# A one-tile expert slot turned and moved, and a port shared by two engines put into a planner's estimates

## The chip, the core and the metric

One core of a Trainium2 chip runs the whole program. Its engines are TensorE (PE, matmuls, with PEld for its weight loads), VectorE (DVE), ScalarE (ACT), GpSimd (POOL) and SyncE (SP, which issues most transfers). The metric is the device time of one execution in microseconds (us); the median of several runs is compared.

## The reference

Three stages, all in float32, each on the output of the one ahead of it:

```python
# 1. linear attention with decay, 4 x 8 heads, 768 steps, 48 wide
cur = einsum('bhd,bhe->bhde', u * kt, vt)
y[:, :, t] = einsum('bhd,bhde->bhe', rt, state + cur)
state = w * state + einsum('bhd,bhe->bhde', kt, vt)
# 2. a dense layer on the 3072 tokens of width 384
h = x @ w_in                      # 384 x 2048
x2 = (h * sigmoid(h)) @ w_out     # 2048 x 384
# 3. each token goes to one of 8 experts (the largest logit)
e_idx = argmax(x2 @ w_gate + modality_bias[modality_id], axis=1)
out[mask] = gate_w * (relu(x2[mask] @ w1[e]) @ w2[e])   # 384 x 1024, 1024 x 384
```

## The kernel before

Every product of stages 2 and 3 is made from three float32r matmuls: a value is split into a high part (h) and the rest (l), and hi*hi, hi*lo and lo*hi are added up. So each product needs ACT for the high part and DVE for the subtraction that gives the low one: xh and xl for inputs, Wh and Wl for weights, gh and gl for the hidden values.

The 3072 tokens are 24 tiles of 128. Attention works tile by tile: POOL makes zb (L448) and scales the keys by a table (L464), DVE scales the queries (L460), PE makes the sums c (L454) and the scores (L487), the output y (L503) and the state (L544). Three tiles make a block of 384 tokens for the dense layer. That has 16 chunks of the hidden width; for a chunk the **first product** is nine matmuls of 384 columns (L618), then ACT takes Silu twice (L622, L623), DVE makes gl (L625), and the **second product** is nine matmuls (L637) into three PSUM banks, one for each tile. While the first two blocks run, the dense weights are converted chunk by chunk on ACT and DVE (L587 to L596). A tile's logits are then computed, tokens are sorted into lists by expert, and rows go to DRAM.

Stage 3 works in nine static **slots**, each with one expert's weights: SP loads them, ACT and DVE split them (L925, L929), POOL gathers the tokens' rows (L915), PE transposes them (L933), and a slot makes 8 first products (L949) with Relu on ACT (L1034) and gl on DVE (L1036), and 8 second products (L957). At its end, outputs are scaled by the gate on DVE and ACT (L963, L961), and POOL writes each tile of 128 rows by an indirect transfer (L966). Eight slots hold 384 tokens; the last, ninth one holds 128 tokens (one tile) and makes its first products in two groups of 36 matmuls of 128 columns. A loop behind them takes what did not fit into the slots (L1079; it does not run here).

What sets the order: `Plan` (L57) collects all operations with an engine, an estimated duration, a priority and dependencies, and `order` (L75) plays them through as a list scheduler: whenever an engine is free in its estimate, the ready operation of least priority starts. The resulting order is written out as it is, and each engine takes its instructions in that order. PSUM banks and buffers are handed out in the same pass. Where the planner finds PE free in the first 150 us of its own estimate, it places a **filler**: four transposes of the identity matrix (L372), which compute nothing that is used. No estimate says that DVE and POOL can hinder each other.

Of the kernel before, what the change touches and what calls it, by code (L numbers as in the profile page):

```python
# [31 lines left out]
NA = 4  # L32
# [20 lines left out]
class Op:  # L53
    __slots__ = ("eng", "dur", "prio", "fn", "deps", "acq", "rel", "lat", "nbytes", "start", "n", "left", "after", "slots")


class Plan:  # L57
# [7 lines left out]
    def add(self, eng, dur, prio, fn, deps=(), acq=(), rel=(), lat=0.2, nbytes=0):  # L65
        o = Op()
        o.eng, o.dur, o.prio, o.fn, o.lat, o.nbytes = eng, dur, prio, fn, lat, nbytes
        o.deps = [d for d in deps if d is not None]
        o.acq, o.rel = list(acq), list(rel)
        o.n, o.after, o.left = len(self.ops), [], 0  # L70
        self.ops.append(o)
        return o

    def order(self):
# [5 lines left out]
        busy = dict.fromkeys(ENGINES, 0.0)  # L80
        events, dma, t, done = [], 0.0, 0.0, []
# [4 lines left out]
        while True:  # L86
            moved = True
            while moved:
                moved = False
                for e in ENGINES:  # L90
# [20 lines left out]
                    busy[e] = t + o.dur  # L111
                    end = t + o.dur + o.lat
                    if o.nbytes:
                        dma = max(dma, t + o.dur) + o.nbytes / 260e3
                        end = dma + 3.8 + o.lat
# [24 lines left out]
def moe_rwkv_kernel(tc, ins, out):  # L140
# [267 lines left out]
    def attention(n):  # L408
# [25 lines left out]
        if n >= NZ:  # L434
            o_pr = add("POOL", 1.2, z - 3.3, lambda: gp.tensor_tensor(nat(0), nat(0), nat(1), op=ALU.mult), [oB])
            o_pu = add("POOL", 1.2, z - 3.0, lambda: gp.tensor_tensor(nat(0), nat(0), UW, op=ALU.mult), [o_pr, o_ul])
# [5 lines left out]
        else:  # L442
# [6 lines left out]
            o_z = add("POOL", 1.4, z - 4, f_z, [oA], acq=[("zb", kz)])  # L449
# [10 lines left out]
        o_r = add("DVE", 0.62, z - 3.0, lambda: vv.tensor_tensor(*scale(0), op=ALU.mult), zd)  # L460
        if n < 3:
            o_k = add("DVE", 0.62, z - 3.0, lambda: vv.tensor_tensor(*scale(1), op=ALU.mult), zd)
        else:
            o_k = add("POOL", 1.4, z - 3.2, lambda: gp.tensor_tensor(*scale(1), op=ALU.mult), zd)  # L464
# [14 lines left out]
        if not last:  # L479
            o_kk = add("POOL", 1.2, z - 2.0, lambda: gp.tensor_tensor(nat(1), nat(1), PKt, op=ALU.mult), [o_pr or oB, o_pk])  # L480
# [65 lines left out]
        if c > 0:  # L546
            st = Sst[b].rearrange("p q a d -> p q (a d)")
            o_sw = add("POOL", 0.95, z - 0.5, lambda: gp.tensor_tensor(st, st, wc.unsqueeze(2).to_broadcast([128, 4, 2 * D]),
                                                                      op=ALU.mult), [sdone[n - B], o_y])
# [21 lines left out]
    def convert(fc):  # L571
# [12 lines left out]
        def cx():  # L584
# [6 lines left out]
                 [o1])  # L591
        o4 = add("DVE", 0.95, z + 0.3, lambda: vv.scalar_tensor_tensor(cx(), cx(), 0x80000000, st_(1),
                                                                      op0=ALU.bitwise_and, op1=ALU.bitwise_or), [o3])
# [578 lines left out]
```

## Time and profile before

| | us |
|---|---|
| median of 3 runs | 781.47 (779.93 to 781.54) |
| the profiled execution | 780.16 |
| its span, from the first to the last instruction | 778.4 |
| PE busy | 763.3 (98%) |
| DVE busy | 400.1 (51%) |
| ACT busy | 341.8 (44%) |
| POOL busy | 214.1 (28%) |

The span starts with the first instruction and ends with the last, and 1.8 us of the execution lie around it. Times in the rows are us from the start of the span. A busy share near 100% says that PE has hardly a gap, and not that what it does is needed: the fillers count as busy. The mean granted clock of TensorE is 0.994 of full speed, so there is a short stretch in which it was lower.

### The profile page before, as it was taken

Reading aid. Unit: us, or ns where it says so; the run is one execution under the profiler, and the core shown is the slowest. Engines: PE = TensorE matmul, PEld = TensorE weight load, DVE = VectorE, ACT = ScalarE, POOL = GpSimd, SP = SyncE. Lnnn points to the kernel's source line nnn. Section 1 sums busy time; section 2 is a strip of 40 time slices with the busy share of each in tenths; the row PEclk is TensorE's granted clock in tenths of the full one; section 3 lists DMA queues with packets and bytes.
Section 4 is the critical chain, followed back from the end, with each engine's and each line's share of the span. In section 5 each row is a group of like instructions: output and inputs, shape, how many; then the busy total and the mean of one; then the engine's idle time right before and its main releaser. Section 6 shows DMA issues by size and latency. Waiting matters only on the chain. (4 is left out here: it accounts for less than half of the span.)

```text
span 778.4 us, 15275 instructions
## 1 busy us (share of the span) xinstructions
PE 763.3 (98%) x6104; PEld 733.9 (94%) x6104; DVE 400.1 (51%) x793; ACT 341.8 (44%) x742; POOL 214.1 (28%) x276
## 2 busy tenths in 40 slices
PE   8989999999999999999999999999999999999996
PEld 7988999999999999999999999999999999999995
DVE  7978985545434433433533442245685455455521
ACT  4756775444434334333433432335643354334410
POOL 4324300343512522342141120321241322222102
PEclk9989999999999999999999999999999999999999
DMA  7625441244311311311022040915265653350000
GB/s 248 217 98 186 167 153 34 89 77 78 92 61 62 93 62 61 93 61 62 24 90 82 22 32 1 377 39 193 82 184 184 223 182 133 133 203 27 11 21 36
DMA packets 23918, 83.24 MB, mean 107 GB/s; under 512 B 7659, under 2 KB 12152, under 8 KB 21538
## 3 DMA queue, kind: packets, MB, share of 16 engines
q1 hardware_dynamic: 19730, 72.55, 28.9%
q0 software_dynamic: 3968, 9.66, 3.7%
q8 instruction: 49, 0.80, 0.5%
q14 instruction: 27, 0.22, 0.2%
q10 hardware_dynamic: 144, 0.00, 0.0%
HBM read 78.92 MB, written 9.77 MB: 114 GB/s over the span
## 5 line engine op out<-in xcount | busy, mean ns | idle before, releaser
L625 DVE TENSOR_TENSOR gl<-sg,gh 128x384 fp32r<-128x384 f32 x128 | 81.0, 633 | 154.5 <-ACT gh L623 146.6
L622 ACT ACTIVATE sg<-ph 128x384 f32<-128x384 f32 x128 | 62.9, 491 | 205.5 <-PE ph L618 187.8
L637 PE MATMUL pa<-Wh,gh 128*128 128x384 f32 x384 | 133.1, 347 | 0.0
L637 PE MATMUL pa<-Wh,gl 128*128 128x384 f32 x384 | 130.0, 338 | 1.2 <-DVE gl L625 1.2
L637 PE MATMUL pa<-Wl,gh 128*128 128x384 f32 x384 | 129.3, 337 | 0.0
L618 PE MATMUL ph<-xh,Wh 128*128 128x384 f32 x384 | 92.9, 350 | 0.0
L618 PE MATMUL ph<-xh,Wl 128*128 128x384 f32 x384 | 88.8, 339 | 0.0
L618 PE MATMUL ph<-xl,Wh 128*128 128x384 f32 x384 | 88.5, 338 | 0.0
L1034 ACT ACTIVATE gh<-ph 128x384 fp32r<-128x384 f32 (+1 forms) x66 | 32.6, 494 | 113.5 <-PE ph L949 107.2
L1036 DVE SCALAR_TENSOR_TENSOR gl<-ph,gh 128x384 fp32r<-128x384 f32 (+1 forms) x66 | 36.8, 558 | 81.2 <-ACT gh L1034 80.4
L637 PEld LDWEIGHTS pa<-Wh,gh 128*128 128x128 f32 x384 | 72.5, 189 | 3.6 <-issue 2.2
L637 PEld LDWEIGHTS pa<-Wh,gl 128*128 128x128 f32 x384 | 72.6, 189 | 1.5 <-DVE gl L625 1.5
L637 PEld LDWEIGHTS pa<-Wl,gh 128*128 128x128 f32 x384 | 72.6, 189 | 0.0
L618 PEld LDWEIGHTS ph<-xh,Wh 128*128 128x128 f32 x384 | 66.2, 189 | 4.4 <-issue 3.0
L475 ACT ACTIVATE atall<-ident,cs 128x128 f32<-128x128 f32 x192 | 62.0, 397 | 18.9 <-DVE cs L457 10.5
L618 PEld LDWEIGHTS ph<-xl,Wh 128*128 128x128 f32 x384 | 69.5, 189 | 0.0
L618 PEld LDWEIGHTS ph<-xh,Wl 128*128 128x128 f32 x384 | 69.5, 188 | 0.0
L929 DVE TENSOR_TENSOR Wl<-raw,Wh 128x1024 fp32r<-128x1024 f32 (+2 forms) x54 | 64.0, 1219 | 9.9 <-ACT Wh L925 9.9
L966 POOL DMA_INDIRECT out_dram<-x2all,it x25 | 33.8, 1354 | 126.6 <-DVE x2all L963 114.7
L957 PE MATMUL pa<-Wh,gh 128*128 128x384 f32 x200 | 67.5, 337 | 1.0 <-DVE x2all L963 0.8
L957 PE MATMUL pa<-Wh,gl 128*128 128x384 f32 x200 | 67.4, 337 | 0.0
L957 PE MATMUL pa<-Wl,gh 128*128 128x384 f32 x200 | 67.0, 335 | 0.0
(225 smaller groups left out, 1285.9 us busy)
## 6 DMA issues: line engine op xcount, KB each, us to landing
raw<-in_we_dram SPq DMA_DIRECT2D x18, 1536.0 KB
AB<-in_av_dram SPq DMA_DIRECT2D x18, 768.0 KB
stall<-in_wio_dram SPq DMA_DIRECT2D x16, 768.0 KB
x_rows<-x2all SPq DMA_DIRECT2D x24, 192.5 KB
AB<-y_slow SPq DMA_DIRECT2D x16, 256.0 KB
stall<-in_av_dram SPq DMA_DIRECT2D x5, 768.0 KB
AB<-in_rk_dram SPq DMA_DIRECT2D x10, 384.0 KB
stall<-in_rk_dram SPq DMA_DIRECT2D x5, 384.0 KB
```

The lines of the kernel that those rows point to most:

```text
L475: act.activation(atb[sl_(kT)][h % 2][:, h // 2, :], ident, AF.Copy, scale=cs[:, h:h + 1])
L618: pe.matmul(p, win(a, fc, kt), (xh, xl)[b_][j % 2][:, kt, :], start=i == 0, stop=i == len(ops) - 1)
L622: o_s = add("ACT", 0.5, s - 4, lambda: act.activation(sgb[sl_(kS)], hps[sl_(kH)][:, 0:n], AF.Silu), [o_g1], acq=[("sg", kS)])
L625: o_l = add("DVE", 0.55, s - 4, lambda: vv.tensor_tensor(glb[sl_(kG)][:, 0:n], sgb[sl_(kS)], ghb[sl_(kG)][:, 0:n].bitcast(F32), op=ALU.sub ...
L637: pe.matmul(a, g[:, ts], wout(wp_, fc), start=begin and i == 0, stop=end and i == 2)
L929: eng.tensor_tensor(e_view(buf, 1)[wi][sl], m2[s]["raw", wi][sl], e_view(buf, 0)[wi][sl].bitcast(F32), op=ALU.subtract)
L957: pe.matmul(a[:, 0:DM], g[:, sl], wt_[:, fc, :], start=fc == 0 and m == 0, stop=fc == NFE - 1 and m == 2)
L966: i = gp.indirect_dma_start(out=out, out_offset=bass.IndirectOffsetOnAxis(ap=m2[s]["it"][:, t:t + 1], axis=0), in_=o, in_offset=None, boun ...
L1034: o2 = add("ACT", 0.62 if small else 0.5, z + k - 6, lambda kH=kH, kG=kG, m=m: act.activation(ghb[sl_(kG)][:, 0:m], hps[sl_(kH)][:, 0:m], ...
L1036: o3 = add("DVE", 0.7 if small else 0.57, z + k - 6, lambda kH=kH, kG=kG, m=m: vv.scalar_tensor_tensor(glb[sl_(kG)][:, 0:m], hps[sl_(kH)][ ...
```

## The change

Three things are done. In `Plan`, an operation can be marked `shared`; when it starts while a marked operation of the other of the two engines DVE and POOL is running in the estimate, its duration there grows by half of the overlap. Marked are the elementwise operations on DVE and POOL of attention, of the weight conversions and of the gl subtraction in the dense layer, and the weight splits of the experts.

The one-tile slot moves from the last place to the one ahead of it (`small` is slot 7 in place of 8), and takes its list entry with it. Its first product is turned: the tokens are the stationary operand and 512 columns of the weights stream past, nine matmuls for half of the hidden width. The result has tokens on partitions, so Relu goes to a tile `hn` in SBUF, PE transposes it in four parts, ACT copies the high part and DVE makes gl.

In the slot that is now the last, the second products of the last two chunks wait for both and are added tile by tile, so that a tile's output need not wait for the other two. The marks alone (`shared=True` at 14 places) are shown at one place:

```diff
@@ order
+        run = dict.fromkeys(ENGINES, 0.0)
...
-                    busy[e] = t + o.dur
-                    end = t + o.dur + o.lat
+                    dur = o.dur
+                    if o.shared:
+                        other = run["POOL" if e == "DVE" else "DVE"]
+                        if other > t:
+                            dur += 0.5 * min(dur if e == "POOL" else 2 * dur, other - t)
+                        run[e] = t + dur
+                    busy[e] = t + dur
+                    end = t + dur + o.lat
@@ attention
-            o_z = add("POOL", 1.4, z - 4, f_z, [oA], acq=[("zb", kz)])
+            o_z = add("POOL", 1.4, z - 4, f_z, [oA], acq=[("zb", kz)], shared=True)
@@ new helpers
+    def e_g1n(buf, xb, k, p):
+        w1h, w1l = e_view(buf, 0)[0], e_view(buf, 1)[0]
+        ops = [(kt, a, b_) for b_, a in ((xh, w1h), (xh, w1l), (xl, w1h)) for kt in range(KT)]
+        for m, (kt, a, b_) in enumerate(ops):
+            pe.matmul(p, b_[xb][:, kt, 0:128], a[:, kt, k * 512:(k + 1) * 512], start=m == 0, stop=m == len(ops) - 1)
+
+    def e_tn(g, p):
+        for i in range(4):
+            pe.transpose(p[:, i * 128:(i + 1) * 128], g[:, i * 128:(i + 1) * 128], ident)
@@ swap
+        pools["hn"] = [ew.tile([128, 512], F32, name=f"hn{i}") for i in range(1)]
@@ expert
-        z = E0 + EU * s
+        z = E0 + EU * s if s < NSTAT - 1 else E0 + EU * (s - 1) + 2.0
-        small = s == NSTAT - 1
+        small = s == NSTAT - 2
+        final = s == NSTAT - 1
+        at_ = NSTAT - 1 if small else NSTAT - 2 if final else s
...
+            if small:
+                kN = ("en", s, k)
+                o1 = add("PE", 2.1, z + k, lambda k=k, kH=kH: e_g1n(buf, xb, k, hps[sl_(kH)]), [o_sp[0, p_] for p_ in range(3)] + o_x,
+                         acq=[("h", kH)])
+                o2 = add("ACT", 0.62, z + k - 6, lambda kH=kH: act.activation(
+                    pools["hn"][0], hps[sl_(kH)], AF.Relu), [o1], rel=[kH])
+                o2 = add("PE", 0.45, z + k - 6, lambda kN=kN: e_tn(pools["hn"][0], tps[sl_(kN)]), [o2], acq=[("t", kN)])
+                o2 = add("ACT", 0.62, z + k - 6, lambda kG=kG, kN=kN: act.activation(ghb[sl_(kG)], tps[sl_(kN)], AF.Copy), [o2],
+                         acq=[("g", kG)])
+                o3 = add("DVE", 0.7, z + k - 6, lambda kG=kG, kN=kN: vv.tensor_tensor(
+                    glb[sl_(kG)], tps[sl_(kN)], ghb[sl_(kG)].bitcast(F32), op=ALU.subtract), [o2], rel=[kN])
...
+            if final and fcs[0] >= NFE - 2:
+                held = [] if fcs[0] == NFE - 2 else held
+                held.append((kG, need))
+                if fcs[0] == NFE - 1:
+                    both = [d for _, ds in held for d in ds]
+                    for t in range(nt_):
+                        def f_g2(t=t):
+                            for i, (kq, _) in enumerate(held):
+                                e_g2(buf, [NFE - 2 + i], t, n, ghb[sl_(kq)], glb[sl_(kq)], aps[sl_(ka[t])])
+                        lastg = last_t[t] = add("PE", 1.05, z + k + 2.3 + 0.1 * t, f_g2, both + [lastg], rel=[kq for kq, _ in held] if t == nt_ - 1 else [])
+                continue
```

What this does to the order is seen at three places. Names in the rows are the program's: pt, ph and pa are PSUM banks, AB_132 the inputs of attention tile 3 and AB_133 those of tile 4, gh_121 and gh_122 the hidden values of chunks 0 and 1. Behind the change, line numbers up to the expert's helpers are 8 higher.

PE, where the second product of chunk 0 ends and attention tile 3 begins (L454 makes c, L487 the scores, L618 is the first product of chunk 3, L637 the second product of chunk 1), before:

```order
L637 MATMUL pa_80<-Wh_73,gl_124 128x384
L454 MATMUL pt_83<-ub,zb_134 128x2 x4
L487 MATMUL pt_82<-AB_132 128x128
L487 MATMUL pt_84<-AB_132 128x128
...
L454 MATMUL pt_83<-ub,zb_135 128x2 x4
L618 MATMUL ph_78<-xh_115,Wh_73 128x384 x3
...
L637 MATMUL pa_81<-Wh_73,gh_122 128x384
```

And with the change (L380 are the fillers, L645 the second product, L462 makes c, L495 the scores, L626 is the first product of chunk 2):

```order
L645 MATMUL pa_80<-Wh_73,gl_124 128x384
L380 MATMUL ph_78<-ident 128x128 x4
L380 MATMUL ph_77<-ident 128x128 x4
...
L645 MATMUL pa_79<-Wh_73,gh_122 128x384
...
L462 MATMUL pt_83<-ub,zb_134 128x2 x4
L495 MATMUL pt_84<-AB_132 128x128
...
L626 MATMUL ph_77<-xh_115,Wh_73 128x384 x3
...
L380 MATMUL ph_78<-ident 128x128 x12
L462 MATMUL pt_83<-ub,zb_135 128x2 x4
```

Five fillers and the second product of chunk 1 now stand ahead of tile 3, and three more fillers between the tiles 3 and 4. In all, 49 fillers are written out in place of 39.

DVE at the same place, from the conversion of chunk 3 (L590, L592, L594, L596 on cx_148) to the scaling of tile 3's queries (L460), before:

```order
L590 TENSOR_SCALAR stall<-cx_148 128x768
L592 SCALAR_TENSOR_TENSOR cx_148<-cx_148,stall 128x768
L625 TENSOR_TENSOR gl_124<-sg_119,gh_121 128x384
L594 ISA cx_148<-stall,cx_148 128x1536
L625 TENSOR_TENSOR gl_125<-sg_120,gh_122 128x384
L460 TENSOR_TENSOR AB_132<-AB_132,Pt 128x512
```

And with the change (all line numbers 8 higher):

```order
L633 TENSOR_TENSOR gl_124<-sg_119,gh_121 128x384
...
L633 TENSOR_TENSOR gl_125<-sg_120,gh_122 128x384
L604 TENSOR_TENSOR Wl_75<-cx_147,Wh_73 128x768
L468 TENSOR_TENSOR AB_132<-AB_132,Pt 128x512
L465 TENSOR_SCALAR cs_480<-pt_83,flag 128x8
L598 TENSOR_SCALAR stall<-cx_148 128x768
L600 SCALAR_TENSOR_TENSOR cx_148<-cx_148,stall 128x768
L602 ISA cx_148<-stall,cx_148 128x1536
```

The gl of chunks 0 and 1 and the queries of tile 3 have come ahead of the conversion of chunk 3.

PE in the one-tile slot, with the change (L964 is its first product, L968 the transposes, L957 the first product of the last slot, L975 second products, the last row here the slot's own):

```order
L964 MATMUL ph_77<-Wh_74,xh_116 128x512 x3
...
L975 MATMUL pa_81<-Wh_73,gh_123 128x384
...
L964 MATMUL ph_78<-Wh_74,xh_116 128x512 x3
...
L968 MATMUL pt_82<-ident,hn_5340 128x128 x4
L975 MATMUL pa_81<-Wh_73,gh_121 128x384
...
L968 MATMUL pt_83<-ident,hn_5340 128x128 x4
L957 MATMUL ph_77<-xh_115,Wh_73 128x384 x3
...
L975 MATMUL pa_80<-Wh_74,gh_122 128x384
```

Before, this slot's 72 narrow matmuls stood at the end of the program, with the second products of the full slot before it between and behind them; now its pieces stand between the products of the full slots on either side.

## Rows read from the trace of the kernel before

**Rows 1.** Stretches: us, busy us (count) of PE, PEld, DVE, ACT, POOL; granted clock; DMA.

```profile
44.00:50.00 6.00, 5.58 (x34) 5.42 (x32) 4.63 (x9) 3.25 (x9) 1.00 (x1) 0.63 0.29 109
76.00:80.00 4.00, 2.85 (x17) 2.64 (x16) 3.96 (x6) 3.70 (x8) 0.88 (x1) 1.00 0.65 240
150.00:552.00 402.00, 401.62 (x3486) 381.09 (x3487) 163.86 (x397) 158.96 (x405) 113.62 (x147) 1.00 0.27 81
```

**Rows 2.** Waits of PE, whole span: us in total, times, longest.

```profile
PE pt L487 <- issue: 1.6, 1, 1.6
PE pa L637 <- DVE gl L625: 1.2, 1, 1.2
```

**Rows 3.** Timeline of PE around 45 us: start, duration, instruction, idle before it.

```profile
41.22 0.95 PE L454 MATMUL pt<-ub,zb 128*128 128x2 f32 x8
...
45.31 1.59 PE L454 MATMUL pt<-ub,zb 128*128 128x2 f32 x8 [0.42 <-DVE cs L457]
46.77 1.31 PE L618 MATMUL ph<-xh,Wh 128*128 128x384 f32 x3
...
49.79 0.52 PE L637 MATMUL pa<-Wh,gh 128*128 128x384 f32 x1
...
52.65 1.08 PE L503 MATMUL pt<-atall,AB 128*32 128x128 f32 x32
```

**Rows 4.** Timeline of PE at a run of four fillers.

```profile
73.82 2.03 PE L372 MATMUL ph<-ident 128*128 128x128 f32 x16
75.61 0.42 PE L637 MATMUL pa<-Wh,gh 128*128 128x384 f32 x1
```

**Rows 5.** Timelines of POOL and DVE, one overlapping pair.

```profile
35.92 1.48 POOL L464 TENSOR_TENSOR AB<-AB,Qt 128x512 f32<-128x512 f32 x1
...
36.30 1.92 DVE L592 SCALAR_TENSOR_TENSOR cx<-cx,stall 128x768 uint32<-128x768 uint32 x1
```

**Rows 6.** DVE by form, 0 to 90 us (busy, mean ns), and two alone.

```profile
L625 DVE TENSOR_TENSOR gl<-sg,gh 128x384 fp32r<-128x384 f32 x9 | 9.2, 1024 | 1.6 <-ACT gh L623 1.6
L590 DVE TENSOR_SCALAR stall<-cx 128x768 uint32<-128x768 uint32 x10 | 8.5, 855 | 0.6 <-ACT cx L587 0.6
...
22.48 0.58 DVE L590 TENSOR_SCALAR stall<-cx 128x768 uint32<-128x768 uint32 x1
...
44.42 0.55 DVE L625 TENSOR_TENSOR gl<-sg,gh 128x384 fp32r<-128x384 f32 x1
```

**Rows 7.** Timeline of PE at the end, the one-tile slot among it.

```profile
752.02 0.69 PE L949 MATMUL ph<-xh,Wh 128*128 128x384 f32 x3
...
753.61 0.33 PE L957 MATMUL pa<-Wh,gh 128*128 128x384 f32 x1
...
755.16 0.44 PE L949 MATMUL ph<-xh,Wh 128*128 128x128 f32 x3
...
759.13 0.39 PE L957 MATMUL pa<-Wh,gh 128*128 128x384 f32 x1
...
766.15 0.34 PE L957 MATMUL pa<-Wh,gl 128*128 128x384 f32 x1
766.63 0.45 PE L957 MATMUL pa<-Wh,gh 128*128 128x384 f32 x1
...
770.73 0.34 PE L957 MATMUL pa<-Wh,gl 128*128 128x384 f32 x1
```

**Rows 8.** Timeline of DVE: the splits for the last slot, and a gl of it.

```profile
729.83 3.50 DVE L929 TENSOR_TENSOR Wl<-raw,Wh 128x1024 fp32r<-128x1024 f32 x3 [0.39 <-ACT Wh L925]
...
759.96 0.69 DVE L1036 SCALAR_TENSOR_TENSOR gl<-ph,gh 128x512 fp32r<-128x512 f32 x1 [5.08 <-ACT gh L1034]
```

**Rows 9.** Timeline of POOL: the last output transfers.

```profile
768.32 0.99 POOL L966 DMA_INDIRECT out_dram<-x2all,it  x1 [0.24 <-issue]
...
769.62 0.99 POOL L966 DMA_INDIRECT out_dram<-x2all,it  x1 [0.24 <-issue]
...
772.01 0.98 POOL L966 DMA_INDIRECT out_dram<-x2all,it  x1 [1.34 <-DVEq L1079]
```

More of the change, by code (lines that the diff above doesn't have):

```diff
@@ L53 @@
 class Op:
-    __slots__ = ("eng", "dur", "prio", "fn", "deps", "acq", "rel", "lat", "nbytes", "start", "n", "left", "after", "slots")
+    __slots__ = ("eng", "dur", "prio", "fn", "deps", "acq", "rel", "lat", "nbytes", "start", "n", "left", "after", "shared")
 class Plan:
@@ L1030, in expert @@
             m = n * step
-            o1 = add("PE", 2.7 if small else 1.57, z + k * (1.0 if small else 1.0), lambda fcs=fcs, kH=kH: e_g1(buf, xb, fcs, n, hps[sl_(kH)]),
-                     [o_sp[0, p_] for p_ in range(3)] + o_x, acq=[("h", kH)])
-            em["g1", s] = em["g1", s] + [o1]
-            o2 = add("ACT", 0.62 if small else 0.5, z + k - 6, lambda kH=kH, kG=kG, m=m: act.activation(
-                ghb[sl_(kG)][:, 0:m], hps[sl_(kH)][:, 0:m], AF.Relu), [o1], acq=[("g", kG)])
-            o3 = add("DVE", 0.7 if small else 0.57, z + k - 6, lambda kH=kH, kG=kG, m=m: vv.scalar_tensor_tensor(
-                glb[sl_(kG)][:, 0:m], hps[sl_(kH)][:, 0:m], 0.0, ghb[sl_(kG)][:, 0:m].bitcast(F32), op0=ALU.max, op1=ALU.subtract),
-                [o2], rel=[kH])
@@ L1039, in expert @@
-            need = [o_sp[1, p_] for p_ in range(((0, 0, 0, 1, 1, 1, 2, 2)[fcs[-1]]) + 1)] + [o3, lastg]
+            if small:
[9 more added lines that the diff above has]
+                    glb[sl_(kG)], tps[sl_(kN)], ghb[sl_(kG)].bitcast(F32), op=ALU.subtract), [o2], rel=[kN])
+            else:
+                o1 = add("PE", 1.57, z + k * 1.0, lambda fcs=fcs, kH=kH: e_g1(buf, xb, fcs, n, hps[sl_(kH)]),
+                         [o_sp[0, p_] for p_ in range(3)] + o_x, acq=[("h", kH)])
+                em["g1", s] = em["g1", s] + [o1]
+                o2 = add("ACT", 0.5, z + k - 6, lambda kH=kH, kG=kG, m=m: act.activation(
+                    ghb[sl_(kG)][:, 0:m], hps[sl_(kH)][:, 0:m], AF.Relu), [o1], acq=[("g", kG)])
+                o3 = add("DVE", 0.57, z + k - 6, lambda kH=kH, kG=kG, m=m: vv.scalar_tensor_tensor(
+                    glb[sl_(kG)][:, 0:m], hps[sl_(kH)][:, 0:m], 0.0, ghb[sl_(kG)][:, 0:m].bitcast(F32), op0=ALU.max, op1=ALU.subtract),
+                    [o2], rel=[kH])
@@ L1049, in expert @@
             o5 = add("ACT" if t == 1 else "DVE", 0.55, z + 1 + 0.1 * t, f_o,
[L1050 removed]
+                     [last_t.get(t, lastg), em.get(("out", s - 2))] + ([routed["sx", NB - 1]] if s < 2 else []), rel=[ka[t]])
             em["out", s] = add("POOL", 1.0, z + 7 + 0.1 * t, lambda t=t: e_out(s, t, x2b[s % 2][:, t, 0:DM]), [o5], lat=5.0)
```

36 lines of the change are left out of this document (18 added, 18 removed).

## The prediction

> **What bounds the kernel now.** I read the windows first: they say where TensorE (PE) is the bound. From 150 to 552 us PE is busy 401.62 of 402 us at full clock [rows 1], so there nothing that ACT, DVE or POOL do shows in the time, and whatever is won or lost on PE before 150 us or behind 700 us is carried to the end one to one. Next the waits of PE. Apart from short ones far behind, where the change leaves the order as it is, PE waits in three places, all before 90 us: 1.6 us ahead of the score matmuls of attention tile 3, 0.42 us ahead of the small matmuls of tile 4, and 1.2 us for a gl [rows 2, 3]. That sum is 3.2 us. Then the timeline of PE around the first two: behind them it runs slowly. [...] Waits and slow clock together cost **6.45 us** in the first 90 us. Everything else there is PE work, and a part of that work is padding: fillers of four transposes each that the planner puts where it believes PE would idle.
>
> Why PE waits at 43 us is seen on DVE and POOL. A POOL multiply runs from 35.92 to 37.40; the DVE operation that begins inside it, at 36.30, takes 1.92 us [rows 5], about 0.97 more than the 0.95 that the plan writes for it. The plan of before knows nothing of this. Over the first 90 us the two forms that lose most are the gl subtraction (9 of them, mean 1024 ns against 0.55 us alone) and the shift of the weight conversion (10, mean 855 ns against 0.58 us) [rows 6]: 9 x 0.47 + 10 x 0.275 = 7.0 us of DVE time that no estimate held.
>
> **The change, part by part.** (1) The estimates. An operation marked as sharing is charged half of its overlap with the other engine's running one. For the pair above the overlap is 1.10 us, so the table now charges 0.55 of the 0.97 that the row shows: 57%. The order that comes out has the same operations, with the second product of chunk 1 moved ahead of tile 3's attention matmuls (they open with c and the scores), and with 49 fillers in place of 39. A group of 16 filler matmuls goes from 73.82 to 75.61 us [rows 4], 0.112 us each; 10 fillers are 40 of them, **4.47 us** more PE work, all before 150 us and so all on the path. From there to the last expert slots the order of PE is the same row by row.
>
> What it can give back is the 6.45 us. Fillers keep PE busy where it now waits, and they let tile 3 come later against its producers. What of it stays is the one unknown; I call it x, the PE waits and slow-clock loss left before 150 us. From below x is 0. From above: the uncharged 43% of the 7.0 us is 3.0 us, if it reaches PE whole, and it can bring the clock down once more for 3.25, so 6.3. Between the two I scale by what happened: of 7.0 us that the plan missed, 3.2 became PE waits (46%), so of 3.0 missed now about 1.4. I take **x = 1.4** without a fall of the clock, because the clock fell only where two waits stand close together; the stretch from 76 to 80 us, with the single 1.2 us wait in it, has a granted clock of 1.00 [rows 1, 2].
>
> The row says that the DVE operation lost 0.97 of 1.10 us of overlap, nearly all. [...]
>
> (2) The one-tile slot, turned. Its first product is now 72 matmuls of 128 columns, in two runs, one of them from 755.16 to 759.13 us and the second as long within 0.01: 7.93 us [rows 7]. It becomes 18 matmuls of 512 columns. The trace has none of that width. If a matmul costs by its columns as the 384-wide ones do (1.59/9 = 0.177 us), one is 0.236 and 18 are 4.24; the least is 0.177 each, 3.2 us; the most is the cost for each column of the narrow ones, 0.110 us for 128, which gives 7.93, no gain. I take 4.24, since 384 is the nearest width. It adds 8 transposes on the identity, the filler's own kind, at 0.112: 0.90. Net **-2.79 us** on PE.
>
> Around it the slot gains a chain: Relu on ACT into the one buffer hn, transposes on PE, copy on ACT, subtraction on DVE. The table writes 0.62 for each ACT step and 0.45 for the transposes, and DVE takes 0.69 us for such a width [rows 8], so 0.62 + 0.45 + 0.62 + 0.69 = 2.4 us and the handovers. The order covers it: between a turned product and the second product that needs its result stand four to five other pieces of 1.55 to 2.1 us. On ACT, Relu and copy stand behind the three conversions of the last slot's first weights, which lie under the second products there; on DVE the three subtractions run 3.50 us from 729.83 [rows 8], and in the new order seven pieces (three second products, two turned ones, two times four transposes: 4.65 + 4.24 + 0.90 = 9.8 us) lie between the first product whose end lets these conversions begin and the last slot's first one. Cover gone, the price is the 2.4 us, twice.
>
> (3) The full slot at the end. Before, PE stands still ahead of the last gl: 766.15 to 766.63 is 0.48 from start to start in place of 0.17 [rows 7], **-0.31 us**. In the new order a second product of 1.55 us lies there. The last two blocks are now added tile by tile, so the three outputs become ready 6 x 0.173 = 1.04 us apart. But POOL writes them at 1.30 us spacing (768.32, 769.62) [rows 9]. With P for the end of PE (771.07 now: the last start at 770.73 and 0.34), the one output of before is issued at P + 0.94 [rows 7, 9]. After, the first is ready 2.08 us earlier, at P - 1.14, and the third issues at P - 1.14 + 2 x 1.30 = P + 1.46: **+0.5 us**. Between nothing and 2.6 us (all three behind one another) this is what the spacing gives.
>
> Sum: x - 6.45 + 4.47 - 2.79 - 0.31 + 0.50 = x - 4.58, with x = 1.4: **-3.2 us**. The profiled execution took 780.16 us, 1.31 under the median of the three runs; so it goes to 777.0, and the median from 781.47 to **778.3 us**.
>
> **The rivals.** *A tight order passes everything on* (slower). The new order puts producers and consumers closer; what is uncharged then reaches PE undamped, and waits with a second one near drop the clock as at 44 us. Price x = 6.3: 781.47 + 1.7 = 783.2. It decides from x = 6.1, where the time is 0.2% over the median. For it: the charge is only 57% of the row's loss, and many DVE results now stand one filler ahead of their use. Against it: DMA arrivals and ACT leave room, and PE has 4.47 us more to run meanwhile. [...]
>
> *The clock falls once, the waits go* (no change): x = 1.4 + 3.25 = 4.7, 781.6. For it: DVE stays close to full until 48 us. Against it: the padding sits just where PE was idle.
>
> *The turned slot gains nothing*, because the wide matmul costs by column what the narrow did or because PE stands in its chain: -3.2 + 2.8 = -0.4, 781.1, no change. Against it: 384 columns cost little more than 128 do now.
>
> *The padding hides everything*: x = 0, 776.9.
>
> **How the numbers follow.** Chances: my forecast 0.52 (its own range 777.0 to 779.9, x from 0.1 to 3.0), no waits left 0.12, the clock falls once 0.13, the turned slot gains nothing 0.09, the tight order 0.14. A measurement of this kernel tells about 0.2% (1.6 us) from no change: faster 0.64 (the first two), same 0.22 (the third and fourth), slower 0.14. The range runs from 776.2 (x = 0, with the output tail at nothing and the matmuls a little cheaper) to 782.9, close under the tight order's full price; what is above and below is about 2 in 10.
>
> **What would show it.** In the changed profile: PE's waits before 100 us sum to some 1.4 us in place of 3.2, and the granted clock from 40 to 56 us stays at the upper level; 196 filler matmuls; the first 512-column matmuls at about 0.236 us from start to start; no PE wait for hn or gl behind 700 us; the last output issued about 1.5 us behind the last matmul. The forecast is wrong if PE waits or slow clock remain in the first 100 us over 3 us, or if the turned slot brings a wait on ACT or DVE that was not there.

## The result and the profile after

The changed kernel takes **788.7 us** in the median of four executions (787.9 to 792.5), the kernel before 781.5 in the same comparison; the ratio is **1.011, with a 95% interval from 1.0084 to 1.0136**. Forecast were 778.3 us and a range up to 782.9. The forecast is wrong, in sign too. The profiled execution took 787.88 us with a span of 786.2, against 780.16 and 778.4 before.

Three places lose time and one gains. The windows of the changed kernel show the first three (us, busy us and count of PE, PEld, DVE, ACT, POOL; then granted clock, DMA share, GB/s):

```profile
40.00:50.00 10.00, 8.45 (x50) 8.08 (x48) 7.66 (x8) 4.27 (x12) 4.76 (x4) 0.66 0.42 155
170.00:190.00 20.00, 16.31 (x143) 15.29 (x143) 6.75 (x13) 5.84 (x17) 6.07 (x6) 0.91 0.36 85
400.00:420.00 20.00, 18.65 (x174) 17.34 (x173) 7.02 (x13) 7.29 (x19) 7.79 (x10) 1.00 0.24 81
```

From 150 to 552 us PE had been busy 401.62 of 402 us before [rows 1]; now two holes stand in that stretch. The waits of PE name them (us in total, times, longest):

```profile
PE pa L645 <- issue: 3.7, 1, 3.7
...
PE pt L495 <- POOL AB L488: 1.5, 1, 1.5
PE pt L511 <- issue: 1.4, 1, 1.4
```

Of the three waits before 90 us [rows 2, 3] one is left, 1.55 us ahead of tile 3's scores. "issue" is time in which PE waited for nothing that the profile shows, and two waits of that kind are new, at 178 and 412 us. PE's timeline at the first place (start, duration, instruction, idle before it):

```profile
39.97 0.95 PE L462 MATMUL pt<-ub,zb 128*128 128x2 f32 x8
42.47 2.08 PE L495 MATMUL pt<-AB 48*128 48x128 f32 x16 [1.55 <-POOL AB L488]
44.48 1.33 PE L626 MATMUL ph<-xh,Wh 128*128 128x384 f32 x3
...
47.52 2.34 PE L380 MATMUL ph<-ident 128*128 128x128 f32 x12
49.70 0.95 PE L462 MATMUL pt<-ub,zb 128*128 128x2 f32 x8
```

Behind the wait PE is slow, as in [rows 3]: the scores take 2.01 us (42.47 to 44.48), the first product 3.04, twelve filler matmuls 2.18. At full clock the same pieces take 1.09, 1.67 and 1.31 (shown below), so the slow clock costs 3.16 us here, beside the wait of 1.55.

And at the second place:

```profile
177.25 0.69 PE L626 MATMUL ph<-xl,Wh 128*128 128x384 f32 x3
181.63 0.34 PE L645 MATMUL pa<-Wh,gh 128*128 128x384 f32 x1 [3.69 <-issue]
...
182.42 0.52 PE L645 MATMUL pa<-Wl,gh 128*128 128x384 f32 x1
...
184.02 1.16 PE L626 MATMUL ph<-xh,Wh 128*128 128x384 f32 x3
...
186.42 0.33 PE L645 MATMUL pa<-Wh,gh 128*128 128x384 f32 x1
```

PE stands 3.69 us, then the second product takes 2.39 us and the first product behind it 2.40, in place of 1.55 and 1.59 [rows 7]: 5.3 us in all.

The end of the program did what it was meant to. PE in the turned slot and its last matmul, then POOL's last output transfers:

```profile
740.10 0.85 PE L964 MATMUL ph<-Wh,xh 128*128 128x512 f32 x3
740.78 0.85 PE L964 MATMUL ph<-Wl,xh 128*128 128x512 f32 x3
...
742.16 0.34 PE L975 MATMUL pa<-Wh,gh 128*128 128x384 f32 x1
...
745.78 0.60 PE L968 MATMUL pt<-ident,hn 128*128 128x128 f32 x4
746.14 0.42 PE L975 MATMUL pa<-Wh,gh 128*128 128x384 f32 x1
...
777.33 0.34 PE L975 MATMUL pa<-Wh,gl 128*128 128x384 f32 x1
```

```profile
776.52 0.98 POOL L984 DMA_INDIRECT out_dram<-x2all,it  x1 [18.83 <-DVE x2all L981]
...
777.81 0.98 POOL L984 DMA_INDIRECT out_dram<-x2all,it  x1 [0.24 <-issue]
...
779.10 0.98 POOL L984 DMA_INDIRECT out_dram<-x2all,it  x1 [0.24 <-issue]
```

Both kernels run the same pieces on PE from 90 us to the expert slots, so the difference of their start times is a running account. How much later than in the kernel before the same piece starts (us):

| place (start in the kernel before) | 12 | 90 | 155 | 191 | 402 | 453 | 716 |
|---|---|---|---|---|---|---|---|
| changed kernel | 0.1 | 2.4 | 3.0 | 8.5 | 9.0 | 10.6 | 10.0 |

PE then ends 6.6 us later (777.67 against 771.07), and the span is 7.8 longer. So the early stretch lost 3 us, the stall at 178 us 5.4, an attention output at 348 us 0.5, the stall at 412 us 1.6, a 0.4 us wait of the kernel before at 509 us is gone, and the end gives 2.2 back.

### The profile page after: what moved, and what is told of

Same layout as the page of the kernel before. It is cut to its first block, busy times and chain, and to the rows that moved or that the text cites. A ratio compares the mean times of both kernels' runs of the same rounds, so it can differ in the third digit from the quotient of the medians.

```text
span 786.2 us, 15264 instructions
## 1 busy us (share of the span) xinstructions
PE 766.9 (98%) x6098; PEld 736.1 (94%) x6098; DVE 397.1 (51%) x793; ACT 342.6 (44%) x744; POOL 215.5 (27%) x276
## 4 chain that ended last, share of the span: by engine, by line
PE 72%; issue 19%; POOL 5%; DMA 2%; SPq 0%; POOLq 0%; DVE 0%; ACT 0%; another core or an unknown queue 0%
PE ph L626 27%; PE pa L645 26%; PE pt L511 5%; POOL out_dram L984 3%; PE pt L495 3%; PE ph L380 2%; PE ph L957 2%; PE pa L975 2%; POOL xgb L923 1%; PE pt L552 1%; PE pt L694 1%; PE ph L313 1%; DMA AB<-in_av_dram 1%; DMA it<-id_list 1%; PE pt L705 1%
## 5 line engine op out<-in xcount | busy, mean ns | idle before, releaser
L633 DVE TENSOR_TENSOR gl<-sg,gh 128x384 fp32r<-128x384 f32 x128 | 77.1, 602 | 159.5 <-ACT gh L631 157.6
L645 PE MATMUL pa<-Wh,gh 128*128 128x384 f32 x384 | 133.0, 346 | 3.7 <-issue 3.7
L645 PE MATMUL pa<-Wh,gl 128*128 128x384 f32 x384 | 129.9, 338 | 0.0
L645 PE MATMUL pa<-Wl,gh 128*128 128x384 f32 x384 | 129.2, 336 | 0.0
L626 PE MATMUL ph<-xh,Wh 128*128 128x384 f32 x384 | 93.5, 352 | 0.0
L626 PE MATMUL ph<-xh,Wl 128*128 128x384 f32 x384 | 89.2, 340 | 0.0
L626 PE MATMUL ph<-xl,Wh 128*128 128x384 f32 x384 | 88.6, 339 | 0.0
L1067 ACT ACTIVATE gh<-ph 128x384 fp32r<-128x384 f32 x64 | 31.4, 491 | 109.4 <-PE ph L957 108.8
L645 PEld LDWEIGHTS pa<-Wl,gh 128*128 128x128 f32 x384 | 72.4, 189 | 3.8 <-issue 3.8
L645 PEld LDWEIGHTS pa<-Wh,gh 128*128 128x128 f32 x384 | 72.3, 188 | 3.0 <-issue 2.0
L1069 DVE SCALAR_TENSOR_TENSOR gl<-ph,gh 128x384 fp32r<-128x384 f32 x64 | 35.4, 554 | 76.9 <-ACT gh L1067 76.7
L645 PEld LDWEIGHTS pa<-Wh,gl 128*128 128x128 f32 x384 | 72.5, 189 | 0.2
L626 PEld LDWEIGHTS ph<-xh,Wh 128*128 128x128 f32 x384 | 66.6, 190 | 4.4 <-issue 2.8
L626 PEld LDWEIGHTS ph<-xh,Wl 128*128 128x128 f32 x384 | 69.9, 190 | 0.0
L626 PEld LDWEIGHTS ph<-xl,Wh 128*128 128x128 f32 x384 | 69.6, 189 | 0.0
L975 PE MATMUL pa<-Wh,gh 128*128 128x384 f32 x200 | 67.4, 337 | 0.8 <-DVE x2all L981 0.8
L975 PE MATMUL pa<-Wh,gl 128*128 128x384 f32 x200 | 67.5, 337 | 0.0
L975 PE MATMUL pa<-Wl,gh 128*128 128x384 f32 x200 | 67.0, 335 | 0.0
```

The lines of the kernel that those rows point to most:

```text
L626: pe.matmul(p, win(a, fc, kt), (xh, xl)[b_][j % 2][:, kt, :], start=i == 0, stop=i == len(ops) - 1)
L633: o_l = add("DVE", 0.55, s - 4, lambda: vv.tensor_tensor(glb[sl_(kG)][:, 0:n], sgb[sl_(kS)], ghb[sl_(kG)][:, 0:n].bitcast(F32), op=ALU.sub ...
L645: pe.matmul(a, g[:, ts], wout(wp_, fc), start=begin and i == 0, stop=end and i == 2)
L975: pe.matmul(a[:, 0:DM], g[:, sl], wt_[:, fc, :], start=fc == 0 and m == 0, stop=fc == NFE - 1 and m == 2)
L1067: o2 = add("ACT", 0.5, z + k - 6, lambda kH=kH, kG=kG, m=m: act.activation(ghb[sl_(kG)][:, 0:m], hps[sl_(kH)][:, 0:m], AF.Relu), [o1], acq ...
L1069: o3 = add("DVE", 0.57, z + k - 6, lambda kH=kH, kG=kG, m=m: vv.scalar_tensor_tensor(glb[sl_(kG)][:, 0:m], hps[sl_(kH)][:, 0:m], 0.0, ghb[ ...
```

## The experiments

### The two halves apart

```diff
-                            dur += 0.5 * min(dur if e == "POOL" else 2 * dur, other - t)
+                            dur += 0.0 * min(dur if e == "POOL" else 2 * dur, other - t)
```

> The slot alone: the changed kernel with the charge for shared time set to nothing, so that the order before the expert slots is that of the kernel before (39 fillers). Theory (the loss is the estimates', the slot does what was forecast): the same waits before 90 us as before, no PE stall at 178 us, and 2.6 us less than before in the same comparison, about 778.9 us. Rival (the slot has a price of its own that the after trace hides): within 1 us of before or slower.

Measured: 776.7 us (775.97 to 777.09) against 780.9, ratio 0.9949 (0.9933 to 0.9966). Once more, with more executions:

> The slot alone once more, in more rounds, since its first comparison (0.9949, 0.9933 to 0.9966) lay a little above the 2.6 us that were forecast for it. Theory (the slot is worth what its rows show, 2.4 us from the last order they share to the end, and the rest is the spread of the start): 0.9960 to 0.9970, 777.5 to 778.5 us. Rival (it is worth more): 0.995 again, under 777 us.

Measured: 777.7 against 780.7, ratio 0.9959 (0.9940 to 0.9978): 3.2 us less (1.7 to 4.7). In the two traces the end gains 2.4 and 2.5 us from the piece at 716 us on. The rest moves from execution to execution: at 12 us the first is 0.9 us ahead of the kernel before, and both lose 0.9 to 1.0 us between 155 and 191 us, 0.3 of them in waits for ACT. The slot is right, and it alone **beats both kernels**. The first trace has no hole like those at 178 and 412 us:

```profile
170.00:190.00 20.00, 19.54 (x182) 17.88 (x181) 8.55 (x19) 7.34 (x19) 5.29 (x6) 1.00 0.55 80
400.00:420.00 20.00, 20.00 (x182) 18.87 (x182) 7.59 (x13) 7.08 (x19) 6.32 (x6) 1.00 0.19 61
```

The second has one at the later place, in the state of an attention tile, and PE has lost 1.8 us by 716 us:

```profile
407.82 0.40 PE L552 MATMUL pt<-AB 128*48 128x48 f32 x8 [1.27 <-issue]
```

So a stall at this place comes in one execution and not in another of one and the same program.

The other half is the kernel before with the first eleven pieces of the diff and the mark at the expert splits:

```diff
-... e_lo(s, buf, wi, p_, vv), [o1])
+... e_lo(s, buf, wi, p_, vv), [o1], shared=True)
```

> The estimates alone: the kernel before with the charge for shared time, without the turned slot. Theory: the PE order up to 700 us is that of the changed kernel, so the 1.5 us wait at 41 us, the slow clock behind it and the 3.7 us stall at 178 us are all here, and the time is before + 10, about 791 us. Rival (the stall at 178 us is an accident of one program image): the stall is not here, 785 to 786.

Measured: 788.3 us, ratio 1.0134 (1.0081 to 1.0188). The whole loss sits in the estimates. Both stalls are there, 3.3 and 2.6 us. But one row contradicts what I had written:

```profile
40.00:50.00 10.00, 8.68 (x73) 8.56 (x74) 9.61 (x13) 5.91 (x14) 3.65 (x3) 1.00 0.32 120
```

PE has the same 1.5 us wait in that window (the waits give `L495` 1.5), and the granted clock is 1.00. In this execution the piece at 155 us starts 1.3 us earlier than before, not 3 later. **The fall of the clock behind the wait at 41 us comes in some executions and not in others of the same order.** In the traces below it comes once more in this order (with id_list held back: a wait of 1.4 us, then 0.66 from 40 to 50 us) and stays away once (without id_list: 1.5 us, then 1.00).

### The wait at 41 us

The waits put it down to POOL's L488. The timelines of DVE and POOL in the changed kernel say something else:

```profile
38.97 2.00 DVE L604 TENSOR_TENSOR Wl<-cx,Wh 128x768 fp32r<-128x768 f32 x1 [0.44 <-ACT Wh L603]
40.89 1.48 DVE L468 TENSOR_TENSOR AB<-AB,Pt 128x512 f32<-128x512 f32 x1
...
40.11 1.71 POOL L488 TENSOR_TENSOR AB<-AB,PKt 128x384 f32<-128x384 f32 x1
```

L468, the scaling of tile 3's queries, ends at 42.37, and PE starts at 42.47. L604 took 2.00 us for the 0.95 that the plan writes, L468 1.48 for 0.62, both across POOL's operations. So the two are exchanged, with a gate in the plan that only lets L604 be picked a little later:

```diff
-..., op=ALU.subtract), [o6], rel=[kX], shared=True)
+..., op=ALU.subtract), [o6] + ([gate(29.0)] if len(cdone) == 2 else []), rel=[kX], shared=True)
```

> The changed kernel with two rows of DVE exchanged: the scaling of tile 3's queries (L468, 40.89 to 42.36 us in the changed kernel) goes ahead of the last conversion step of chunk 2 (L604, 38.97 to 40.96). Every other row on every engine stays. Theory (the 1.55 us PE wait at 41 us ends with L468, which two overlaps with POOL made late, not with POOL's L488 that the waits name): L468 ends at about 40.4, the wait is gone or under 0.2 us, the clock does not fall from 42 to 50 us, and PE is 1.5 us (wait) to 4.7 us (wait and slow clock) earlier at 60 us; the stall at 178 us stays. Rival (POOL's L488 or another is what ends the wait): a wait of 1 to 1.5 us and the slow clock stay.

Measured: 785.9 us, ratio 1.0077 (1.0053 to 1.0101). The wait is gone and the clock stays; DVE, then PE, then the window:

```profile
38.10 0.69 DVE L468 TENSOR_TENSOR AB<-AB,Pt 128x512 f32<-128x512 f32 x1
38.70 2.06 DVE L604 TENSOR_TENSOR Wl<-cx,Wh 128x768 fp32r<-128x768 f32 x1
```

```profile
39.56 0.95 PE L462 MATMUL pt<-ub,zb 128*128 128x2 f32 x8
40.44 1.16 PE L495 MATMUL pt<-AB 48*128 48x128 f32 x16
41.53 0.79 PE L626 MATMUL ph<-xh,Wh 128*128 128x384 f32 x3
...
43.20 1.47 PE L380 MATMUL ph<-ident 128*128 128x128 f32 x12
44.51 0.95 PE L462 MATMUL pt<-ub,zb 128*128 128x2 f32 x8
```

```profile
40.00:50.00 10.00, 10.00 (x83) 9.83 (x83) 9.83 (x13) 6.38 (x15) 4.87 (x3) 1.00 0.40 148
```

The piece at 155 us starts 2.2 us earlier than before, 5.2 earlier than in the changed kernel (1.55 + 3.16 of them by the rows above, 0.4 from the start). POOL's L488 was only the last name on the list. The stall at 178 us stays (3.9 us), as expected.

```diff
-                            dur += 0.5 * min(dur if e == "POOL" else 2 * dur, other - t)
+                            dur += 1.0 * min(dur, other - t)
```

> The changed kernel with the whole overlap charged in place of half of it. Theory (half is too little, by rows where a DVE operation loses nearly all of its overlap): PE waits before 100 us under 0.5 us and no slow clock there, some more fillers, and PE at 100 us is no later than in the changed kernel. Rival (a larger charge only trades waits for fillers): waits go, but PE at 100 us is later by the extra fillers, 0.45 us each. What happens at 178 us is open in both, since the order of POOL and DVE changes.

Measured: 779.4 us, ratio 0.9981 (0.9957 to 1.0004). Charging the whole overlap gives 54 fillers; the waits of attention tile 3 and the gl are gone, one of 0.8 us for DVE is new at 21 us, the clock is 1.00 from 30 us on. At 155 us PE is 1.5 us later than before: the five more fillers cost 2.2, so this is a trade, and a poorer one than the exchange of two rows. Charging half of the overlap left the 1.5 us wait, charging all of it none. That a DVE operation takes longer beside POOL's is in the trace of the changed kernel (L468 1.48 us at 40.89 across L488, 0.68 at 46.59 with POOL idle); what the two engines share, a port or something else, no run shows. There is no stall at 178 us in this order.

### The stalls at 178 and 412 us

What else happens there? Around 178 us other engines wait as well. DVE's operation on a result that PE had finished at 174.6 starts only at 182.10, and its releaser is not seen:

```profile
182.10 0.72 DVE L567 TENSOR_TENSOR S<-pt,S 48x192 f32<-48x192 f32 x2 [8.61 <-remote]
```

The DMA view from 172 to 184 us has one packet of the kind "instruction" (packets, MB, share of 16 engines): 1.5% of 16 x 12 us are 2.9 us for 16 KB.

```profile
q8 instruction: 1, 0.02, 1.5%
```

The whole run has 49 such packets on that queue for 12,196 matmuls and weight loads of PE: one for each 249. Most of the others take 0.9 to 1.4 us. That they bring PE's program is an inference from the count: DVE has 793 instructions in this trace, ACT 744 and POOL 276. Whether PE stands at 178 us for want of instructions is the question then. The DMA view of 175 to 176 us alone, in which the packet starts (17.6% of 16 us are 2.8):

```profile
q8 instruction: 1, 0.02, 17.6%
```

So the packet ends about when PE stops (177.94), not when PE goes on.

And the kernel before has the same disturbance, where nobody asked what it was: SP needs 4.92 us to issue one transfer, and ACT gets the first product that PE had finished at 174.9 at 178.06.

```profile
172.81 4.92 SPq L425 DMA_DIRECT2D AB<-y_slow  x1
```

```profile
178.06 0.49 ACT L622 ACTIVATE sg<-ph 128x384 f32<-128x384 f32 x1 [4.56 <-PE ph L618]
```

PE lost nothing then. Ahead of it, in both kernels, POOL writes three lists of 128 single numbers, the id_list transfers of the first group; in the changed kernel they are issued from 165.75 to 169.49:

```profile
168.51 0.97 POOL L788 DMA_INDIRECT id_list<-ids_c,r_si  x1 [0.23 <-issue]
```

Two suspicions follow: these transfers make everything slow for a while, and PE then runs out of instructions. For the first, they are held back:

```diff
-... f_sc, [o_si], lat=9.0)
+... f_sc, [o_si] + ([gate(175.0)] if j == 0 else []), lat=9.0)
```

> The changed kernel with the three id_list transfers of the first group (POOL, 165.75 to 169.49 us) held back by about 20 us. PE's and SP's rows are the same word for word. Theory C (the slow stretch at 169 to 185 us follows these scatters of 4-byte rows): PE's stall at 178 us is gone, 782 to 783 us, and a slow stretch comes behind the scatters' new place at about 190 to 205 us. Rival D (the slow stretch has nothing to do with them): stall of 3.7 us at 178 us as before, 788 us.

Measured: 783.3 us (778.2 to 790.2 in ten executions), ratio 1.0010 (0.9988 to 1.0033). In the trace, one with a fallen clock at 41 us, PE passes 178 us without a hole, and the instruction packet there takes 0.5% x 16 x 12 = 0.96 us:

```profile
q8 instruction: 1, 0.02, 0.5%
```

```profile
182.20 1.29 POOL L788 DMA_INDIRECT id_list<-ids_c,r_si  x1 [0.17 <-issue]
```

The next packet, at 191.1 us, takes 3.8 us: the slow stretch has moved with the transfers. PE does not stop in that one, but loses 1.2 and 2.4 us in attention outputs (L511) at 214 and 407 us, behind the second and the fifth group. Then the transfers are left out of both kernels altogether (the output then lacks the experts' rows; only what lies before 550 us is read):

```diff
-                apart(id_s, gp.indirect_dma_start(
-                    out=idl, out_offset=bass.IndirectOffsetOnAxis(ap=T_["si"][:, t], axis=0), in_=ids_c[:, n:n + 1],
-                    in_offset=None, bounds_check=NE * SLOT - 1, oob_is_err=False))
+                gp.memset(junk, 0.0)
```

> The changed kernel without the 24 id_list transfers (POOL's small operation behind each stays; the expert slots then gather padding rows, so only what lies before 552 us is to be read). PE's rows are the same. Theory C (transfers and signals are slow for some 15 us behind each group of three such scatters, and PE's stalls at 178 and 412 us lie in such stretches): both stalls are gone, instruction packets of PE take about 1 us all through 150 to 450 us, and PE at 420 us is 6 to 9 us earlier than in the changed kernel. Rival D: slow transfers or stalls remain.

> The kernel before without the 24 id_list transfers, to be read up to 550 us only. Theory C: the slow stretch at 172.6 to 182.5 us goes (SP's transfer at 172.81 took 4.92 us to issue, ACT waited to 178.0), but PE had lost nothing in it, so PE at 500 us is within 0.5 us of the kernel before. With the run of the changed kernel without these transfers it says what the estimates are worth when nothing stalls. Rival: PE gains more than 1 us here too.

Measured: the changed kernel without them 779.1 us, ratio to the kernel before 0.9973 (0.9953 to 0.9993); the kernel before without them 781.4, ratio 0.9999 (0.9984 to 1.0014). Both stalls are gone, no instruction packet of the changed kernel from 165 to 550 us takes over 1.4 us, and PE is 1.3 us ahead of the kernel before at 155, 191, 402 and 453 us alike, where the changed kernel is 3.0 to 10.6 behind. All that is left of PE's waits from 12 to 550 us:

```profile
PE pt L495 <- POOL AB L488: 1.5, 1, 1.5
```

So **where nothing stalls and the clock stays up, the estimates gain about what was forecast for them**: without the transfers PE is 1.3 us ahead with the change and 0.9 without it, 0.4 us between them, for a forecast of 0.6 (6.45 - 4.47 - 1.4). The kernel before had lost nothing in the slow stretches of its trace. The ten executions of the changed kernel stand in two groups, 777.3 to 778.1 and 780.0 to 781.4. That the second group is those with a fallen clock at 41 us (3.16 us) is an inference from the distance; one of them was traced, in the first group, at a clock of 1.00.

For the second suspicion PE's program is renumbered. A first try put 55 tiny matmuls into the warm-up in place of 14 of its 50 transposes, 82 instructions more with their weight loads. The expectation was made for 70 and 112; PE runs 17.3 matmuls and weight loads a us from 150 to 552 us [rows 1], so 112 are some 6 us, and the packet would start at about 169 us in place of 175.09:

```diff
-    for _ in range(50):
+    for _ in range(30):
+        pe.matmul(hps[1][0:32, 0:4], ones[:, 0:32], ones[:, 0:4], start=True, stop=True)
+    for i in range(36):
         pe.transpose(hps[1][:, 0:128], ident, ident)
+        if i > 10:
+            pe.matmul(hps[1][0:32, 0:4], ones[:, 0:32], ones[:, 0:4], start=True, stop=True)
```

> [...] Theory A (PE runs out of instructions, because the packet that starts at 175.09 takes 2.8 us in place of 0.95 and falls into a stretch in which all transfers are slow): the packet moves to about 169 us, the 3.7 us stall and the slow clock behind it go, 788 - 5.5 = about 783 us. Rival B (PE waits there for a result or a semaphore): stall of 3 to 4 us at 178 us as before, 788 us.

Measured: 793.1 us, ratio 1.0156 (1.0139 to 1.0173). The warm-up spoilt the comparison: alternating the two kinds kept a transpose at 0.52 us, so the work began 8.3 us later than in the changed kernel and was 13.7 us behind at the first attention output. Behind that the 178 us stall is not there; the one at 412 is, at the same matmuls of the same attention output, 1.7 us, and the last instruction packet ahead of it had ended 9 us before. Inconclusive for the first, and against the suspicion for the second.

The clean test is in the kernel before. Up to 550 us its PE program has the same instructions as the changed one but for 40 transposes, with their weight loads 80 instructions, and from 155 us on in the same order. It gets 40 tiny matmuls, ahead of the warm-up, where PE waits for its first data; the changed kernel gets 88, 176 instructions, which together with its 80 make 256, about one packet by the count above (249):

```diff
+    for _ in range(40):
+        pe.matmul(hps[1][0:32, 0:4], ones[:, 0:32], ones[:, 0:4], start=True, stop=True)
     for _ in range(50):
         pe.transpose(hps[1][:, 0:128], ident, ident)
```

> The kernel before with 40 tiny bf16 matmuls (32 x 4) ahead of the warm-up, in the 2 us in which PE waits for its first data: 80 instructions, as many as the changed kernel's 40 filler transposes have with their weight loads. Nothing else moves. Theory A (a stall depends on which of PE's instructions have to be fetched in the slow stretch behind the id_list transfers, that is on the numbering of PE's program): the kernel before now has the stalls of the changed kernel, 3 to 4 us ahead of the second product at 175 us and 1 to 2.5 us in the attention output at 402 us, with slow clock behind the first, and takes 785 to 788 us. Rival (the stall is a matter of the changed order of POOL, DVE and SP): no stall, 781 us.

> The changed kernel with 88 such tiny matmuls, 176 instructions: with the 80 of its extra fillers 256, after which PE's program is again divided as in the kernel before. They take about 2.8 us where 2.1 us are free, so the start may be some 0.7 us later. Theory A: no stall at 178 and at 412 us, 780 to 783 us (the upper end where the clock falls behind the wait at 41 us). Rival: stalls as in the changed kernel, 788 to 789 us.

Measured: the kernel before with 80 instructions more takes **786.8 us**, ratio 1.0099 (1.0062 to 1.0135); the changed kernel with 176 more takes **780.4**, ratio 1.0005 (0.9983 to 1.0026). The first now has the stall, inside the first product, two matmuls ahead of where the changed kernel has it, and a slow instruction packet ahead of it (1.6% x 16 x 12 = 3.1 us):

```profile
172.80 0.34 PE L620 MATMUL ph<-xl,Wh 128*128 128x384 f32 x1
177.06 0.99 PE L620 MATMUL ph<-xl,Wh 128*128 128x384 f32 x2 [3.92 <-issue]
177.85 0.52 PE L639 MATMUL pa<-Wh,gh 128*128 128x384 f32 x1
```

```profile
q8 instruction: 1, 0.02, 1.6%
```

PE stops in the middle of a product: the matmuls ahead of the stop had already read both of its operands, xl and Wh, so no other engine's result was due there. At the attention output, where 1 to 2.5 us were expected, only 0.3 us are lost.

The second has lost it, and keeps 1.4 us at the attention output:

```profile
170.00:190.00 20.00, 20.00 (x169) 18.84 (x160) 9.41 (x17) 8.82 (x23) 5.43 (x7) 1.00 0.71 109
```

Nothing but the number of PE's instructions ahead of the place was changed, in either direction, and the stall at 178 us came and went with it. The times do not overlap: none of the four executions with 80 more is under 784.8 us, and none of the 19 of the kernel before is over 783.3. The packets moved too: in the kernel before they start at 164.9 and 184.1 us, ahead of the slow stretch and behind it; with 80 more one starts at 170.5, inside it; in the changed kernel with 176 more they are at 165.7 and 185.1 again, 0.8 and 1.0 us later, where PE's pieces are 1.2 and 1.1 later. That the work begins 1.0 us earlier with the 80 is not the reason: the slot alone begins 0.9 earlier too, and has no such stall. Last, the same with the exchange of two DVE rows:

> The same 88 tiny matmuls in the kernel that has tile 3's queries scaled ahead of the conversion step (no wait at 41 us, no slow clock there). Theory A: no PE stall at all before 550 us, 777 to 778 us, in every execution (no execution with a fallen clock at 41 us). Rival: stalls as without the tiny matmuls, 785 us.

Measured: 777.9 us (775.6 to 781.8), ratio 0.9982 (0.9960 to 1.0004). There is no wait at 41 us, no stall at 178, and 0.9 us left at the attention output. The median is as expected; the executions spread over 6 us, where 777 to 778 in every one was expected. It is no better than the slot alone.

How far PE is from the kernel before at the same pieces, in all these traces (us later, minus is earlier):

| kernel | 12 | 90 | 155 | 191 | 402 | 453 |
|---|---|---|---|---|---|---|
| changed | 0.1 | 2.4 | 3.0 | 8.5 | 9.0 | 10.6 |
| slot alone | -0.9 | -1.2 | -1.2 | -0.2 | -0.2 | -0.2 |
| estimates alone | -1.0 | -1.95 | -1.3 | 3.7 | 3.7 | 7.9 |
| two DVE rows exchanged | -0.3 | -2.8 | -2.2 | 4.1 | 4.5 | 8.5 |
| whole overlap charged | 0.0 | -1.2 | 1.5 | 1.45 | 1.45 | 1.45 |
| id_list held back | -0.2 | 1.8 | 2.5 | 2.4 | 4.4 | 8.8 |
| changed, no id_list | -0.9 | -1.9 | -1.25 | -1.3 | -1.3 | -1.3 |
| before, no id_list | -0.7 | -0.8 | -0.8 | -0.9 | -0.9 | -0.9 |
| before, 80 more | -1.0 | -1.6 | -1.4 | 4.0 | 4.5 | 4.95 |
| changed, 176 more | -0.7 | 0.55 | 1.2 | 1.1 | 1.1 | 2.95 |
| exchanged, 176 more | -0.7 | -3.3 | -2.6 | -2.7 | -2.7 | -1.3 |

**What stays open.** A slow instruction packet alone does not stop PE: with the whole overlap charged one took 3.1 us at 171.2, in the same slow stretch, and PE went on. And where PE stops near 178 us (four traces), it does so within 0.5 us of the packet's end, and stands 3.1 to 3.7 us beyond it. Whether the news of the landed packet comes late, as other news do in these stretches (182.10 us for a result of 174.6), or the next packet is what is missing, the traces do not show, nor how far ahead PE holds its instructions. The stall at the attention output (412 us) hangs on the id_list transfers, since it goes with them. That the numbering makes it is not shown: it is there with 176 instructions more, smaller; it is not in the trace of the kernel before; and the slot alone, with that kernel's numbering, has one at 407 us in one trace of two. At 214 us, with id_list held back, PE stood 1.2 us in an attention output with no instruction packet in the 9 us ahead. Whether PE lacks instructions there or something else holds it was not settled. And why three lists of single numbers make other transfers slow for some 15 us is not shown by any run.

## Why the prediction was wrong, step by step

**"From there to the last expert slots the order of PE is the same row by row."** That is so, and the step that failed stands on it: I took the same order for the same time, put the stretch from 150 us to the slots at nothing, and left out that 40 more matmuls renumber everything behind them. The stretch lost 7.0 of the 10.0 us by which PE is late at 716 us: 5.4 at 178 us, which the numbering brings and takes away, and 1.6 at 412 us, which needs the id_list transfers and whose cause is open. No rival had it. The trace of before showed the disturbance, on SP and ACT, and I read PE's busy 401.62 of 402 us [rows 1] as room without risk.

**x, and the clock.** "I take x = 1.4 without a fall of the clock, because the clock fell only where two waits stand close together." The wait was well sized, 1.55 us. The reason for leaving the clock out was wrong: a single 1.55 us wait was followed by 3.16 us of slow clock, so x was 4.7 in the profiled execution, the rival "the clock falls once" to the digit. Behind the 3.69 us stall it fell again (0.91 over 170 to 190 us). At the place of the first fall it came again behind a wait of 1.4 us (id_list held back), and for a shorter time behind one of 1.1 us (changed, 176 more: 0.83 over 40 to 50 us). In two other traces with a wait of 1.5 us at the same place it did not fall, and there the early stretch gained, as forecast. With three falls in five traces it deserved a chance near one half, not 0.13. The 3.25 us of slow clock in the 6.45 are three differences of start times in the kernel before [rows 3, 7]: 3.02 us behind the waits against 1.59 at the end for a first product, 2.86 against 1.55 for a second one, 1.46 against 0.95 for eight small matmuls; the granted clock was 0.63 from 44 to 50 us [rows 1]. The 0.95 is the length of a row; from start to start the eight take 0.81 at full clock (44.51 to 45.32 in the kernel with the exchanged rows), so their loss was 0.65 and not 0.51, and the 6.45 us were 6.6.

**Which operation ends the wait.** The prediction named the gl and the conversion as what DVE loses; it was the query scaling behind a conversion step, and the exchange of the two showed it. The scaling is missing from the prediction's 7.0 us, though the same view of the kernel before has it at 988 ns where the plan writes 0.62:

```profile
L460 DVE TENSOR_TENSOR AB<-AB,Pt 128x512 f32<-128x512 f32 x6 | 5.9, 988 | 0.8 <-DVEq L348 0.8
```

So DVE lost more than 7.0 us to the overlaps. This leaves x = 1.4 as it was, since x is 43% of the 3.2 us of waits whatever the sum is, but the upper bound of 6.3 was too low.

**The fillers.** 16 of them go from 45.32 to 47.02 us in the kernel with the exchanged rows, 0.106 us each for a forecast 0.112. Right.

**The turned slot.** A 512-column matmul takes 0.229 us from start to start (2.06 / 9, 740.10 to 742.16) for a forecast 0.236; four transposes take 0.36 for 0.45. So 18 x 0.229 + 0.72 = 4.84 us stand in place of 7.93, -3.09 for -2.79, and no PE wait for hn or gl stands behind 700 us. The rival "the turned slot gains nothing" is out, and the wait ahead of the last gl [rows 7] is gone.

**The output tail.** The last transfer is issued at P + 1.43 (779.10 against 777.67) for a forecast P + 1.46 and P + 0.94 before [rows 9]. But the span ends 8.53 us behind P, before it was 7.33, so the tail costs 1.2 us for a forecast 0.5: behind the last issue the program takes 7.1 us in place of 6.4, which I had left out. The end as a whole gave 2.2 us where 2.6 were forecast.

**The tight order** was to pass uncharged loss on to PE by waits. The time came out slower, as that rival had it, and beyond its 783.2 us, but not by its mechanism: of its x = 6.3, 3.0 us were waits on DVE and POOL, and before 100 us these sum to 1.55; most of the loss lies behind 150 us.

## What to carry to other kernels

A stretch in which PE never waits is not safe from a change that leaves its order alone: here 80 PE instructions more at the start brought an instruction packet into the slow stretch (170.5 us), 176 more took it out of there in the changed kernel (165.7 and 185.1), and this was worth 6 to 7 us with no other row changed. Before a gain of a few us is believed or given up, look for stretches in which several engines wait for nothing visible, ask what transfer came ahead of them, and shift PE's program by some tiny matmuls to see whether the time hangs on the numbering. And price a PE wait of 1.5 us as the wait, with the slow clock behind it as an even chance (three of five traces of this order), and look at the operations that end last before believing the name that the wait carries.

## What the runs showed that was not expected

- Behind groups of three id_list transfers (128 numbers each) other transfers are slow, for some 15 us behind the first group: instruction packets of 16 KB take up to 3.8 us in place of about 1, one transfer takes 4.92 us to issue, and DVE and ACT start on results of PE up to 7 us late (174.6 to 182.10 and 174.9 to 178.06 us). Held back by 16 us, the transfers took the slow stretch along.
- PE can stand 3.7 us without any recorded wait. 80 instructions more at the start bring such a stall into the kernel before (786.8 us in place of 779.8), 176 more take it out of the changed one.
- A wait of 1.4 to 1.55 us on PE at one place was followed by a granted clock of 0.66 over 40 to 50 us in two traces and of 1.00 in two others.
- Tiny matmuls alternating with transposes made a poor warm-up: each transpose took 0.52 us with its tiny matmul, against 0.16 in a plain one, and the eight small matmuls behind it took 1.56 us in place of 0.82. The granted clock of these stretches reads 1.00, so the rows do not say why.
- From start to start, at a granted clock of 1.00, an fp32r matmul took 0.229 us here for 512 columns (740.10 to 742.16 for nine), 0.177 for 384 and 0.110 for 128 [rows 7].
